# Softmax attention and soft experts on one core: denominators inverted on GpSimd, and one copy moved from ScalarE to VectorE

## The chip, the core and the metric

The kernel runs on one core of a Trainium2 chip. Its time is the device time of one execution in microseconds (us); the time before is the median of three runs. The engines are called as in the profile: PE is TensorE, PEld its weight loads, DVE is VectorE, ACT is ScalarE, POOL is GpSimd, SP is SyncE. Each engine works through its own queue in order and waits at semaphores for the others.

## What is computed

The reference is attention with an extra one in the denominator, followed by a soft mixture of experts on its output.

```python
scores = scale * np.matmul(q, k.transpose(0, 1, 3, 2))      # 8 x 12 heads, 448 tokens, 64 wide
m = np.max(scores, axis=-1, keepdims=True)
e = np.exp(scores - m)
attn = e / (np.sum(e, axis=-1, keepdims=True) + np.exp(-m) + 1e-09)
x = np.matmul(attn, v)                                      # to 3584 x 768
logits = x @ phi                                            # 32 slots
d = softmax of logits over tokens; slot_input = d.T @ x
slot_out = relu(slot_input @ w1[e]) @ w2[e]                 # 8 experts, 4 slots each
out = (softmax of logits over slots) @ slot_out
```

Only the division by attention's denominator and the maxima m of the last heads are touched by the change.

## The kernel before

**Pairs and groups.** The 96 heads are worked in 48 pairs, n = 0 to 47, six pairs to a batch element. The loop over s from 0 to 47 issues the work of several pairs mixed: scores and exponentials of pair s (`AB`, `Bk`), row maxima of later pairs (`A`, `A1`), the product of the probabilities with v for pairs s and s - 1 (`AV`), the normalization of pair s - 1 (`N1`, `N2a`, `N2b`), the transposes of pair s - 2 (`PX`) and, once in six pairs, the steps of the mixture's softmax (`P`). The order within a step is written out by hand in lists of tokens (L700): in a steady step it is 'AB0', 'AV3', 'AB1', 'AVd', 'AVc', 'N1', 'PO0', 'AB2', 'N2a', 'H', 'N2b', 'PO1', 'W', 'AVa', 'PX', 'AVb', 'PO2', 'PO3', 'G'. Since every engine's queue is in order, that list sets who stands behind whom.

**Row maxima.** PE writes scores into PSUM (L302, L294, L284), and DVE reduces each 128x448 tile to a column (L303, L296, L287). When all pairs of a group (three pairs, fewer at the start) have their columns, PE turns them (`W2`, L310 and L313), ACT copies the turned rows from PSUM to `mT` (`W3`, L319) and makes exp(-m) from the columns into `ec` (L324). The scores of the group's pairs then get their maxima subtracted on PE by a second matmul (L380, L354) which reads `mT`, and ACT takes the exponential from PSUM (L382, L357). There are 17 groups; the last is pairs 45 to 47, and its `W3` is issued in step 44.

**Normalization.** v carries a column of ones, so the product with v also gives the sum of e. `N1` copies the product from PSUM to `ubuf` (ACT, L435; DVE for the last pairs). `N2a` adds 1e-9 and `ec` to the sums: one DVE instruction of 128x7 into `rec` (L447). `N2b` inverts `rec` (DVE, L454) and scales: one product of 128x384 (L457) and two of 64x64 (L468). `on_pool(n)` is true for n under 44, and there the products are POOL's; for the last four pairs they are DVE's (ACT has a part in the very last). Between L447 and L454 the list has 'H', which puts one row maximum (L296) and, in two pairs of three, a copy of turned q and k (L265) on DVE's queue.

**After it.** `PX(n)` transposes the normalized pair on PE (L484), one step after its `N2b`; ACT or DVE copies the result to `xT` (L494, L492, L490), and POOL doubles 64 columns (L495).

**What else is on POOL's queue.** The copies of v into the layout with ones (L397 to L400, each third step), the issues of the loads of q and k (L161) and v (L165, L166), of the experts' weights (L111, L131) and of a copy of weights within DRAM (L137), two or three small steps per batch element of the mixture's softmax (L547, L562, L579), and memsets at the start (L217 to L219).

Of the kernel before, what the change touches and what calls it, by code (L numbers as in the profile page):

```python
# [8 lines left out]
F32 = mybir.dt.float32  # L9
# [3 lines left out]
ALU = mybir.AluOpType  # L13
# [19 lines left out]
def kernel(  # L33
# [10 lines left out]
    nc = tc.nc  # L44
    B, H, S, D = q.shape
# [16 lines left out]
    const = ctx.enter_context(tc.tile_pool(name="const", bufs=1))  # L62
# [7 lines left out]
    identf = const.tile([128, 128], F32, name="identf")  # L70
    ident2 = const.tile([128, 128], BF16, name="ident2")
    ones = const.tile([128, 2], BF16, name="ones")
    blocks = const.tile([128, 4], BF16, name="blocks")
    sel = const.tile([128, NP], BF16, name="sel")
    phi_sb = const.tile([128, KC, NS], BF16, name="phi_sb")
# [67 lines left out]
    with ExitStack() as at:  # L143
# [72 lines left out]
        for t in xb:  # L216
            nc.gpsimd.memset(t[:, 3, :], 0.0)  # L217
        nc.gpsimd.memset(ones, 1.0)
        nc.gpsimd.memset(ones[64:128, 1:2], 0.0)  # L219

        ec, mT, eT, av, us = {}, {}, {}, {}, {}
        qkT = {}
        st = {"e2": 0}
# [46 lines left out]
        groups = [range(0, 1), range(1, 3), range(3, 6), range(6, 9), range(9, 12), range(12, 15), range(15, 18), range(18, 21), range(21, 24), range(24, 27), range(27, 30), range(30, 33), range(33, 36), range(36, 39), range(39, 42), range(42, 45), range(45, 48)]  # L270
# [45 lines left out]

        def W3(g):
            t = psm.tile([128, S], BF16, tag="mT", name="mT")
            nc.scalar.copy(t, st["ps_m"][:, 0:S])  # L319
            mT[g] = t  # L320
            e = psm.tile([128, NP, 4, 2], F32, tag="ec", name="ec", bufs=3)
            w = wm[g % 2][:, 0:512].rearrange("p (i c) -> p i c", i=4)
            for h in range(2):
                nc.scalar.activation(e[:, :, :, 1 - h].rearrange("p l i -> p i l"), w[:, :, 64 * h:64 * h + NP],  # L324
                                     AF.Exp, scale=-scale)
            ec[g] = e
# [99 lines left out]
        on_pool = lambda n: n < NPAIR - 4  # L426
# [23 lines left out]
        def N2b(n):  # L450
            b, pb = divmod(n, PB)
            u, rec = us[n], recs[n]
            eng = nc.gpsimd if on_pool(n) else nc.vector
            nc.vector.reciprocal(rec, rec)  # L454
            x = xb[b % 2]
            c = pb * 128
            eng.tensor_mul(  # L457
                x[:, 0:3, c:c + 128].rearrange("p i (h d) -> p i h d", h=2),
                u[:, 0:6, 0:D].rearrange("p (i h) d -> p i h d", h=2),
                rec[:, 0:6].rearrange("p (i h) -> p i h", h=2).unsqueeze(3).to_broadcast([128, 3, 2, D]))  # L460
            if n == NPAIR - 1:
                for h in range(2):
                    r, d = slice(64 - 64 * h, 128 - 64 * h), slice(c + 64 * h, c + 64 * h + 64)
                    nc.scalar.mul(x[r, 3, d], st["av3"][r, 0:D], rec[r, 6:7])
                return
            for h in range(2):
                r, d = slice(64 - 64 * h, 128 - 64 * h), slice(c + 64 * h, c + 64 * h + 64)
                eng.tensor_mul(x[r, 3, d], u[r, 6, 0:D], rec[r, 6:7].to_broadcast([64, D]))  # L468
# [259 lines left out]
        warm(2, 512, 64)  # L728
        W2(0)
        W3(0)  # L730
        As(1)
        T(2)
# [20 lines left out]
        def do(tok, s):  # L753
# [3 lines left out]
            elif tok == "AV3":  # L757
                for i in range(4):
                    AV(s - 1, i, [3])
            elif nm == "AV":  # L760
                i = "abcd".index(tok[2])
                AV(s - i // 2, i, range(3))
            elif tok == "H":
                Bk(s, 3, 1, turned(s + 6, (12, 12, 4)) if s < NPAIR - 6 else ())
            elif tok == "N1":
                N1(s - 1)
            elif tok == "N2a":
                N2a(s - 1)
            elif tok == "N2b":
                N2b(s - 1)  # L770
            elif tok == "PX":
                PX(s - 2)
            elif tok == "W":
                while wnext[0] < len(groups) and (not runs or runs[0][0] > groups[wnext[0]][-1]):
                    W2(wnext[0])
                    W3(wnext[0])
                    wnext[0] += 1
            elif nm == "PO":
                step(s, int(tok[2]))
            elif tok == "G":  # L780
                while later:
                    later.pop(0)()
            elif tok == "X":
                prep()
            elif tok == "P6":
                PX(n6)

        for s in range(NPAIR):
# [3 lines left out]
            for y in range(2 * (s < 3)):  # L792
# [21 lines left out]
                if y == 0:  # L814
                    if s:
                        for i in (2, 3):
                            AV(s - 1, i, range(3))
                        for i in range(4):
                            AV(s - 1, i, [3])
                        N1(s - 1)  # L820
                else:
                    if early and s:
                        N2a(s - 1)
                    if hs > 1:
                        do("W", s)
                    AV(s, 0, range(3))
                    if s == 2:
                        PX(s - 2)
                    if s:
                        N2b(s - 1)  # L830
                    AV(s, 1, range(3))
                    do("G", s)
# [3 lines left out]
            g = (s + 10) // 3  # L836
# [3 lines left out]
            g = (s + 9) // 3  # L840
# [22 lines left out]
        n = NPAIR - 1  # L863
# [6 lines left out]
        N1(n)  # L870
        N2a(n)
        N2b(n)
        nc.gpsimd.memset(mine, 0.0)
        for g in range(2):
# [181 lines left out]
```

## Time and profile before

| | us |
|---|---|
| runs | 287.29, 288.33, 289.04; median 288.33 |
| profiled execution | 287.19, of which the span of instructions is 285.4 |
| busy in the span | PE 262.8, ACT 243.4, DVE 248.4, POOL 191.1 |
| L303, row maxima on DVE | 254 of 0.612 |
| L382, exponentials on ACT | 272 of 0.608 |
| L454, reciprocals on DVE | 48 of 0.187 |
| L447, denominators on DVE | 47 of 0.173 |
| L457, products on POOL | 44 of 0.824; before them POOL was idle for 27.2 in all |
| L468, products on POOL | 88 of 0.287 |
| L319, copies of maxima on ACT | 17 of 0.558 |

A line of the timeline has the start and the length in us, the engine, the line of the kernel, the operation, the tiles written and read with their shapes, and a count if several were merged; in brackets stands how long the engine was idle before it and who ended that. A line of the windows has, for each engine, the busy time in the stretch and the number of instructions; PEclk is the granted clock of TensorE. An instruction's length is not always what it costs its queue: DVE and ACT start the next instruction up to 0.2 us before the last has ended, so costs to a queue are read from start to start. Most of R is one big SBUF buffer that holds many tiles by turns.

### The profile page before, as it was taken

What the parts mean: (1) busy time and instruction counts of PE and PEld (TensorE: products, weight loads), DVE (VectorE), ACT (ScalarE), POOL (GpSimd) and SP (SyncE); (2) the same over time, 40 slices, a digit from 0 to 9 for tenths busy, and PEclk for the clock granted to TensorE, in tenths of its full rate; (3) what the DMA queues carried; (4) which work ended last, traced back from release to release, by engine and by line L of the source; (5) the groups of instructions that cost most, each with busy time, mean ns of one, the idle gap of its engine ahead of it and who ended that gap; (6) DMA issues with size and microseconds to landing.
All of it is one profiled execution on the core that took longest, in us unless ns stands there. A gap on an engine that the chain in (4) does not pass through costs nothing.

```text
span 285.4 us, 11963 instructions
## 1 busy us (share of the span) xinstructions
PE 262.8 (92%) x4967; PEld 151.4 (53%) x4967; DVE 248.4 (87%) x587; ACT 243.4 (85%) x556; POOL 191.1 (67%) x387
## 2 busy tenths in 40 slices
PE   8998999999999999999999999999899999995800
PEld 3455565656565656555665656556555466542100
DVE  6999999999999999999999999999899687438900
ACT  3688999999999999999999999999899996456800
POOL 8868697979688989878888888897757743000000
PEclk9999999999999999999999999999999999998555
DMA  7999999999999999999999999999947999939994
GB/s 135 166 184 157 203 206 205 200 208 181 184 195 209 176 190 201 207 198 172 133 205 162 194 204 209 177 201 203 179 61 110 148 164 233 364 142 364 422 434 199
DMA packets 50214, 57.67 MB, mean 202 GB/s; under 512 B 2928, under 2 KB 42608, under 8 KB 49776
## 3 DMA queue, kind: packets, MB, share of 16 engines
q0 software_dynamic: 45280, 42.29, 95.0%
q1 hardware_dynamic: 4880, 14.62, 13.2%
q8 instruction: 39, 0.64, 0.8%
q14 instruction: 15, 0.12, 0.1%
HBM read 88.18 MB, written 14.16 MB: 359 GB/s over the span
## 4 chain that ended last, share of the span: by engine, by line
PE 60%; DVE 22%; POOL 6%; issue 3%; ACT 3%; DVEq 0%; POOLq 0%
DVE R L303 13%; PE ps_av L422 10%; PE ps_a L302 9%; PE ps_b L377 6%; PE ps_b L380 6%; PE ps_t L237 3%; PE ps_av L414 3%; PE ps_x L484 3%; DVE R L296 2%; PE ps_b L348 2%; PE ps_warm L179 2%; PE ps_o L943 2%; PE ps_so L915 2%; PE ps_l L515 2%; PE ps_h L900 2%
## 5 line engine op out<-in xcount | busy, mean ns | idle before, releaser
L303 DVE TENSOR_REDUCE R<-ps_a 128x1 bf16<-128x448 f32 x254 | 139.9, 612 | 1.7 <-PE ps_a L302 1.1
L382 ACT ACTIVATE R<-ps_b 128x448 bf16<-128x448 f32 x272 | 135.0, 608 | 2.6 <-PE ps_b L380 2.0
L302 PE MATMUL ps_a<-R 64*128 64x448 bf16 x254 | 89.9, 354 | 0.1
L377 PE MATMUL ps_b<-R 64*128 64x448 bf16 x272 | 70.6, 354 | 0.0
L380 PE MATMUL ps_b<-mT,sel 64*128 64x448 bf16 x272 | 68.5, 349 | 0.2 <-ACT mT L319 0.2
L422 PE MATMUL ps_av<-R 128*128 128x65 bf16 (+1 forms) x1248 | 64.7, 196 | 0.6 <-issue 0.4
L422 PEld LDWEIGHTS <-R 128*128 128x128 bf16 (+1 forms) x1248 | 46.7, 101 | 24.1 <-issue 21.9
L457 POOL TENSOR_TENSOR R<-ubuf,rec 128x384 bf16<-128x384 f32 x44 | 36.2, 824 | 27.2 <-DVE rec L454 12.6
L357 ACT ACTIVATE R<-ps_b 128x448 bf16<-128x448 f32 x64 | 37.5, 603 | 2.7 <-PE ps_b L354 2.5
L237 PE MATMUL ps_t<-ident,R 64*64 64x64 bf16 x1344 | 31.1, 195 | 0.3 <-DVE R L287 0.2
L380 PEld LDWEIGHTS <-sel 64*128 64x128 bf16 x272 | 23.9, 94 | 11.2 <-issue 1.6
L468 POOL TENSOR_TENSOR R<-ubuf,rec 64x64 bf16<-64x64 f32 x88 | 25.3, 287 | 6.8
L296 DVE TENSOR_REDUCE R<-ps_a 128x1 bf16<-128x448 f32 x48 | 29.5, 614 | 0.0
L237 PEld LDWEIGHTS <-R 64*64 64x64 bf16 x1344 | 26.3, 110 | 3.4 <-issue 1.6
L302 PEld LDWEIGHTS <-R 64*128 64x128 bf16 x254 | 23.7, 93 | 7.2
L435 ACT COPY ubuf<-ps_av 128x455 f32<-128x455 f32 x44 | 26.6, 604 | 0.0
L494 ACT CAST R<-ps_x 128x448 bf16<-128x448 f32 x41 | 25.0, 611 | 0.0
L348 PE MATMUL ps_b<-R 64*64 64x448 bf16 (+1 forms) x112 | 21.6, 369 | 0.6 <-DVE R L287 0.6
L354 PE MATMUL ps_b<-mT,sel 64*64 64x448 bf16 (+1 forms) x112 | 20.5, 350 | 1.3 <-issue 1.0
L287 DVE TENSOR_REDUCE R<-ps_a 128x1 bf16<-128x448 f32 x34 | 18.7, 614 | 0.7 <-PE ps_a L284 0.6
L951 DVE TENSOR_SCALAR W<-ps_o,ubuf 128x768 f32<-128x768 f32 (+2 forms) x21 | 14.8, 746 | 4.5 <-PE ps_o L943 2.1
L484 PE MATMUL ps_x<-ident,R 128*128 128x128 bf16 x192 | 17.8, 213 | 0.1
(163 smaller groups left out, 470.8 us busy)
## 6 DMA issues: line engine op xcount, KB each, us to landing
W<-in_moe_w_dram POOLq DMA_DIRECT2D x22, 768.0 KB, 10.2
R<-in_v_dram POOLq DMA_DIRECT2D x32, 192.0 KB, 5.6
out_dram<-W SPq DMA_DIRECT2D x2, 2688.0 KB, 10.9
R<-in_q_dram POOLq DMA_DIRECT2D x14, 336.0 KB, 8.9
R<-in_k_dram POOLq DMA_DIRECT2D x14, 336.0 KB, 9.9
wd<-in_moe_w_dram POOLq DMA_DIRECT2D x8, 384.0 KB, 9.9
R<-wd SPq DMA_DIRECT2D x8, 384.0 KB, 7.2
out_dram<-W SPq DMA_DIRECT2D x6, 384.0 KB, 2.9
```

The lines of the kernel that those rows point to most:

```text
L237: nc.tensor.transpose(ps[r, a, c:c + 64], nat["qk"[a], n // NP][f, n % NP, tok * D:(tok + 1) * D], ident[f, f])
L296: nc.vector.reduce_max(top(n, i), ps[:, 0:S], axis=AX.X)
L302: nc.tensor.matmul(ps[:, 0:S], t[r, 0, i * 128:(i + 1) * 128], t[r, 1, :], start=True, stop=True)
L303: nc.vector.reduce_max(top(n, i, hl), ps[:, 0:S], axis=AX.X)
L348: nc.tensor.matmul(outs[hl], t[rs[hl], 1, cols], t[rs[hl], 0, :], start=True, stop=False)
L357: nc.scalar.activation(e, p[:, 0:S], AF.Exp, scale=scale)
L377: nc.tensor.matmul(ps[hl][:, 0:S], t[rs[hl], 1, cols], t[rs[hl], 0, :], start=True, stop=False)
L380: nc.tensor.matmul(ps[hl][:, 0:S], sel[rs[hl], pl:pl + 1].to_broadcast([64, 128]), mT[mg(n)][rs[hl], :], start=False, stop=True)
L382: nc.scalar.activation(e[:, hl, :], ps[hl][:, 0:S], AF.Exp, scale=scale)
L422: nc.tensor.matmul(o, eT[n, i, hl][:, qc], vh[:, h, :], start=(i == 0 and (u == 0 and hl == 0 or u == 3 and n == NPAIR - 1)), stop=(i == 3 ...
L435: (nc.scalar.copy if n1_act(n) else nc.vector.tensor_copy)(u, src)
L457: eng.tensor_mul(x[:, 0:3, c:c + 128].rearrange("p i (h d) -> p i h d", h=2), u[:, 0:6, 0:D].rearrange("p (i h) d -> p i h d", h=2), rec[: ...
```

## The change

The reciprocal of the first 44 pairs goes from DVE to POOL, where it is written as a power: `rec` to the minus one, with the exponents in a tile `minus` of 128x7, set once at the start. It is issued where L454 stood, just ahead of POOL's products. The last four pairs keep DVE's reciprocal. And for the last of the 17 groups the copy of the turned maxima from PSUM is DVE's instead of ACT's.

```diff
+    minus = const.tile([128, 7], F32, name="minus")
...
         nc.gpsimd.memset(ones, 1.0)
+        nc.gpsimd.memset(minus, -1.0)
...
         def W3(g):
             t = psm.tile([128, S], BF16, tag="mT", name="mT")
-            nc.scalar.copy(t, st["ps_m"][:, 0:S])
+            (nc.vector.tensor_copy if g == len(groups) - 1 else nc.scalar.copy)(t, st["ps_m"][:, 0:S])
...
             eng = nc.gpsimd if on_pool(n) else nc.vector
-            nc.vector.reciprocal(rec, rec)
+            if on_pool(n):
+                nc.gpsimd.tensor_tensor(rec, rec, minus, op=ALU.pow)
+            else:
+                nc.vector.reciprocal(rec, rec)
```

## The prediction

> **What bounds the kernel now.** I read the page first, for the totals and for the chain of work that ended last.
>
> ```profile
> PE 262.8 (92%) x4967; PEld 151.4 (53%) x4967; DVE 248.4 (87%) x587; ACT 243.4 (85%) x556; POOL 191.1 (67%) x387
> ...
> PE 60%; DVE 22%; POOL 6%; issue 3%; ACT 3%; DVEq 0%; POOLq 0%
> ```
>
> Three engines are nearly full, and the chain changes between PE and DVE. POOL looks free at 67%, but the chain has 6% on it. So I read the windows next, in one stretch of the attention loop:
>
> ```profile
> core 0: us, PE busy (x) PEld busy (x) DVE busy (x) ACT busy (x) POOL busy (x), PEclk, DMA share, GB/s
> ...
> 121.00:147.00 26.00, 26.00 (x546) 15.65 (x543) 25.52 (x62) 25.78 (x62) 21.25 (x44) 1.00 1.13 174
> ```
>
> Here DVE, ACT and PE leave less than 0.5 us of 26 idle (POOL's 21.25 counts its DMA issues). The loop takes about 4.6 us a pair (from the first L457 at 26.4 to the 44th at 224.8: 198.4 us for 43 pairs), so POOL is free for 4.75 / 5.7 = 0.8 us a pair. Then the timeline of POOL and DVE in one cycle of three pairs, because V's copies and the loads come in cycles of three:
>
> ```profile
> 138.41 0.81 POOL L457 TENSOR_TENSOR R<-ubuf,rec 128x384 bf16<-128x384 f32 x1
> ...
> 140.08 0.80 POOL L111 DMA_DIRECT2D W<-in_moe_w_dram  x1
> 141.59 0.82 POOL L457 TENSOR_TENSOR R<-ubuf,rec 128x384 bf16<-128x384 f32 x1 [0.71 <-ACT ec L324]
> ...
> 145.21 0.54 POOL L562 TENSOR_TENSOR z<-lb,lb 128x160 f32<-128x160 f32 x1
> 146.56 0.83 POOL L457 TENSOR_TENSOR R<-ubuf,rec 128x384 bf16<-128x384 f32 x1 [0.82 <-DVE rec L454]
> ```
>
> ```profile
> 140.12 0.15 DVE L447 SCALAR_TENSOR_TENSOR rec<-ubuf,ec 128x7 f32<-128x7 f32 x1
> 140.19 0.61 DVE L296 TENSOR_REDUCE R<-ps_a 128x1 bf16<-128x448 f32 x1
> 140.72 0.61 DVE L265 COPY R<-ps_t 128x896 bf16<-128x896 bf16 x1
> 141.25 0.18 DVE L454 RECIPROCAL rec<-rec 128x7 f32<-128x7 f32 x1
> 141.36 0.23 DVE L532 TENSOR_REDUCE cm<-lb 128x4 f32<-128x128 f32 x1
> ```
>
> See two things. The reciprocal stands 0.5 to 1.1 us behind the denominator's sum (L447), since a row maximum and, in two pairs of three, a copy are queued between them; it is the reciprocal, not ACT's `ec` of the label, that ended the wait at 141.59 (it ended at 141.43). And the first product of the cycle did not wait at all: POOL came to it 1.3 us late (the reciprocal ended at 137.05), behind V's copies and three DMA issues. Who waits for POOL is in the timeline of the next cycle:
>
> ```profile
> 153.78 0.82 POOL L457 TENSOR_TENSOR R<-ubuf,rec 128x384 bf16<-128x384 f32 x1
> 154.67 0.64 POOL L468 TENSOR_TENSOR R<-ubuf,rec 64x64 bf16<-64x64 f32 x2
> 155.37 0.10 PEld L484 LDWEIGHTS <-R 128*128 128x128 bf16 x1 [0.23 <-POOL R L468]
> ```
>
> PE's fourth transpose of that pair stood until POOL had finished. In the other late pairs the same transposes start 0.5 to 2.1 us after POOL's last product, mostly about 1 us.
>
> **Part one, what DVE loses.** 44 of the 48 reciprocals go (n from 0 to 43; the last four stay on DVE). Each is 0.18 us long, but DVE starts its next instruction 0.11 us after it (141.25 to 141.36). 44 x 0.107 = 4.7 us of DVE's queue. Were DVE the path throughout, all of it would come; were ACT or PE, nothing: 0 to 4.7. In the loop's stretch from 43 to 199 us the chain lies on DVE for about 30% (L303 24.1%, L296 3.8%, L265 and small ones the rest). I take 30% of 4.7 = 1.4 us.
>
> **Part one, what POOL gains.** 44 powers of 128x7, in front of each product. The trace has none. Call P the time that one adds to POOL's queue. From below: POOL's products take 0.287 us at 64 columns and 0.824 at 384, so 1.68 ns a column over 0.18 us; at 7 columns 0.19. The product reads what the power wrote; a copy over a fresh memset (L852, L855) starts 0.07 us after its end. P is at least 0.26. By ratio: POOL against DVE on the same products is 0.287 / 0.220 = 1.30 and 0.824 / 0.558 = 1.48; times the reciprocal's 0.187 that is 0.24 to 0.28, with the gap 0.31 to 0.35. The arithmetic of a power beyond that is not in any row; the longest computation on POOL, 0.92 us, is the upper end that I keep. I take 0.35, nearest to the ratio.
>
> What hides it: the power waits for L447 rather than for L454, so POOL starts earlier wherever it waited. In the cycle shown, L447 had ended (140.27) before POOL came free (140.88), so all of the 0.71 but the usual 0.07 is recovered; at 146.56 the sum ended at 145.78 and POOL was free at 145.75, so 0.82 less 0.15 of signalling. Together 1.3 us in three pairs, 0.43 to 0.45 a pair. While 3P is under that, lateness does not pile up. At 0.35 it does not; only the pair at 153.78, which has no cover, pays about 0.3 us. Above 0.45 each pair adds P - 0.45 to POOL's lateness until the transposes wait each cycle: about 44 x (P - 0.45), less the 1 us of slack that is used up once.
>
> Behind the waiting power on POOL's queue stand the product, L495, the copies of V and the issues of q, k, v and the weights. They stood behind the waiting product already. V's copies are used two pairs later and the loads later still; that is their cover, and without it they would join the same lateness. The memset of `minus` (0.1 us, by L218 and L219) falls into POOL's 0.43 us wait at 11.44: nothing.
>
> **Part two, the last copy of maxima.** From the timeline:
>
> ```profile
> 224.47 0.24 PE L313 MATMUL ps_m<-ident,R 128*128 128x64 bf16 x2
> 224.82 0.55 ACT L357 ACTIVATE R<-ps_b 128x448 bf16<-128x448 f32 x1
> 225.25 0.55 ACT L319 CAST mT<-ps_m 128x448 bf16<-128x448 f32 x1
> 225.39 0.29 DVE L556 TENSOR_REDUCE lb<-ps_bc 128x32 f32<-128x128 f32 x1 [0.76 <-PE ps_bc L555]
> 225.85 0.36 PE L380 MATMUL ps_b<-mT,sel 64*128 64x448 bf16 x2 [0.20 <-ACT mT L319]
> ```
>
> The transposed maxima are in PSUM at 224.71. On ACT the copy stands behind an exponential and ends at 225.80, and PE waits 0.20 for it. DVE is idle from 224.63 to 225.39; its copy of 128x455 took 0.63, so it ends near 225.40, just when L556 could start. That gives PE the 0.20 and ACT 0.41 (the step from L319 to L324) in a stretch where ACT has no idle time: 0.2 to 0.4. I take 0.2.
>
> **Sum.** -1.4 - 0.2 + 0.3 = -1.3 us. The profiled execution took 287.19 us (span 285.4 and 1.8 around it), so 285.9. The median of the runs is 288.33, 1.1 above; with the same step, 287.0.
>
> **The rivals.** (a) *POOL becomes the bound* because a power costs more than 0.45 us. For it: a power is no single product, and POOL is already late once in each cycle. Against it: both ratios. At P = 0.6 the loss is 44 x 0.15 - 1 = 5.6, and what DVE gave is worth nothing: 294 on the median's scale. At 0.9 it is 18.8: 307. If the power is worked through at many times a product's cost, say 2 us, it is 67: 355. This one is slower, with its turn at P = 0.45. Chance 0.40, of which 0.17 beyond 0.9 and 0.04 too small to tell.
>
> (b) *DVE was the bound nearly everywhere*: PE's pieces in the chain are waits for PSUM that DVE frees. For it: reductions follow each other without a gap. Against it: ACT is as full. All 4.7 and 0.4 come: 283.2. Chance 0.08.
>
> (c) *The first power costs extra once*, its code being brought in. The 2.4 us between the first pair's last product and its transposes (28.00 to 30.42) hide as much; beyond that each us adds one. The nearest row is ACT's table load, 1.28 us, which would be hidden, and the first L457 (0.82) was no longer than the rest. For it to matter it must take twice the cover, 4.8 us: then 289.4. Chance 0.05. The Trainium skill's GPSIMD Engine Reference, section 2.1, says that the first call to a freshly loaded kernel pays some 6 us that the profile does not show as an instruction. By that the sum, as an estimate, would be 3.5 us higher, near 290.5. No run here shows it.
>
> **Chances.** The forecast, P from 0.26 to 0.45 with DVE's part between little and most, has 0.47. A difference of 0.5%, about 1.4 us, is what a measurement of this kernel can tell. The forecast lies close to that bound, so I split it: 0.28 faster, 0.19 within. With the rivals: faster 0.28 + 0.08 = 0.36; within 0.19 + 0.04 + 0.05 = 0.28; slower 0.36. The range goes from (b), 283.2, to P = 0.9, 307; the forecast's own range is 284.5 to 288.3.
>
> **What would show it.** In the profile after, the power's row on POOL gives P less its gap; L457 should still show waits before it, now ended by L447; DVE should have 44 instructions fewer and about 4.7 us less work; L484 should wait for L468 no more than once or twice; L380's wait for `mT` near 225 should be gone. I am wrong on the sign if the power takes over 0.4 us, if POOL stands near 100% in the windows, or if PE's weight loads wait for L468 in each cycle.

## The result, and the profile after

The changed kernel takes 334.56 us (median of 4, 332.56 to 335.27) against 288.15 for the kernel before: a ratio of 1.160, 95% interval 1.154 to 1.165, or 46 us slower. The range on record ended at 307. In the changed kernel the line numbers are 1 to 5 higher: the power is L457, the products are L462 and L473, the transposes of `PX` L489, POOL's doubling of 64 columns L500, the mixture's logits L520.

From the page of the changed kernel: the totals, the chain, and the row of the power.

```profile
PE 277.7 (83%) x4966; PEld 157.2 (47%) x4967; DVE 253.6 (76%) x544; ACT 249.2 (75%) x555; POOL 259.4 (78%) x432
...
POOL 40%; PE 32%; DVE 9%; ACT 7%; issue 7%; POOLq 0%; DVEq 0%; ACTq 0%
...
L457 POOL TENSOR_TENSOR rec<-rec,minus 128x7 f32<-128x7 f32 x44 | 66.4, 1509 | 2.9 <-DVE rec L449 0.8
```

POOL's share of the chain went from 6% to 40%. One power of seven columns takes 1.51 us; the reciprocal on DVE took 0.187. Of the 27.2 us that POOL waited ahead of its products, 2.9 are left ahead of the powers and 3.5 ahead of the products. The window of the same stretch as before:

```profile
121.00:147.00 26.00, 21.39 (x402) 12.78 (x396) 18.79 (x41) 19.43 (x46) 24.72 (x41) 0.87 1.09 167
```

DVE, ACT and PE, which had been full, now each idle for 4.6 to 7.2 us of 26, and POOL is the full one. Who waits for it, from POOL's timeline and PE's row at 133 us:

```profile
128.90 0.79 POOL L138 DMA_DIRECT2D wd<-in_moe_w_dram  x1
129.76 1.51 POOL L457 TENSOR_TENSOR rec<-rec,minus 128x7 f32<-128x7 f32 x1
131.35 0.82 POOL L462 TENSOR_TENSOR R<-ubuf,rec 128x384 bf16<-128x384 f32 x1
132.25 0.65 POOL L473 TENSOR_TENSOR R<-ubuf,rec 64x64 bf16<-64x64 f32 x2
132.86 0.23 POOL L500 COPY R<-R 128x64 bf16<-128x64 bf16 x1
133.14 0.21 PE L520 MATMUL ps_l<-phi_sb,R 128*128 128x32 bf16 x1 [3.89 <-POOL R L500]
```

From the power's start to the product's it is 1.59 us: that is what one power adds to POOL's queue. The queue runs without a gap here, and at the end of six of the eight batch elements PE stands until POOL's last doubling: 18.0 us in six waits at L520 (before, at L515, a single weight load waited for POOL, for 0.2 us), beside 12.6 at the transposes L489. From POOL's first 128x384 product to its 44th it is 246.8 us instead of 198.4: the loss lies in the loop.

### The profile page after: what moved, and what is told of

It is laid out like the page before. It is cut to its first block, busy times and chain, and to the rows that moved or that the text cites. A ratio compares the mean times of both kernels' runs of the same rounds, so it can differ in the third digit from the quotient of the medians.

```text
span 332.8 us, 12012 instructions
## 1 busy us (share of the span) xinstructions
PE 277.7 (83%) x4966; PEld 157.2 (47%) x4967; DVE 253.6 (76%) x544; ACT 249.2 (75%) x555; POOL 259.4 (78%) x432
## 4 chain that ended last, share of the span: by engine, by line
POOL 40%; PE 32%; DVE 9%; ACT 7%; issue 7%; POOLq 0%; DVEq 0%; ACTq 0%
POOL rec L457 11%; POOL R L462 6%; POOL R L473 6%; PE ps_av L424 5%; PE ps_a L304 4%; PE ps_b L379 3%; DVE R L289 3%; POOL W L112 3%; PE ps_b L382 3%; POOL R L162 3%; ACT R L384 2%; DVE R L305 2%; POOL R L166 2%; PE ps_so L920 2%; PE ps_h L905 2%
## 5 line engine op out<-in xcount | busy, mean ns | idle before, releaser
L305 DVE TENSOR_REDUCE R<-ps_a 128x1 bf16<-128x448 f32 x254 | 142.1, 619 | 18.9 <-PE ps_a L304 9.9
L384 ACT ACTIVATE R<-ps_b 128x448 bf16<-128x448 f32 x272 | 133.4, 578 | 15.2 <-PE ps_b L382 13.7
L304 PE MATMUL ps_a<-R 64*128 64x448 bf16 x254 | 94.2, 371 | 0.2 <-DVE R L298 0.2
L379 PE MATMUL ps_b<-R 64*128 64x448 bf16 x272 | 75.6, 370 | 1.0 <-DVE R L298 1.0
L382 PE MATMUL ps_b<-mT,sel 64*128 64x448 bf16 x272 | 73.5, 366 | 0.0
L457 POOL TENSOR_TENSOR rec<-rec,minus 128x7 f32<-128x7 f32 x44 | 66.4, 1509 | 2.9 <-DVE rec L449 0.8
L424 PEld LDWEIGHTS <-R 128*128 128x128 bf16 (+1 forms) x1248 | 49.4, 105 | 25.1 <-issue 22.6
L462 POOL TENSOR_TENSOR R<-ubuf,rec 128x384 bf16<-128x384 f32 x44 | 36.4, 827 | 3.5
L359 ACT ACTIVATE R<-ps_b 128x448 bf16<-128x448 f32 x64 | 36.2, 583 | 1.9 <-PE ps_b L356 1.6
L489 PE MATMUL ps_x<-ident,R 128*128 128x128 bf16 x192 | 22.1, 225 | 13.7 <-POOL R L462 6.6
L473 POOL TENSOR_TENSOR R<-ubuf,rec 64x64 bf16<-64x64 f32 x88 | 25.5, 290 | 6.7
L298 DVE TENSOR_REDUCE R<-ps_a 128x1 bf16<-128x448 f32 x48 | 29.6, 617 | 0.0
L520 PE MATMUL ps_l<-phi_sb,R 128*128 128x32 bf16 x192 | 7.5, 177 | 18.0 <-POOL R L500 18.0
L489 PEld LDWEIGHTS <-R 128*128 128x128 bf16 x192 | 13.2, 102 | 18.7 <-POOL R L473 9.1
```

Of the source, the lines that this page charges most:

```text
L304: nc.tensor.matmul(ps[:, 0:S], t[r, 0, i * 128:(i + 1) * 128], t[r, 1, :], start=True, stop=True)
L305: nc.vector.reduce_max(top(n, i, hl), ps[:, 0:S], axis=AX.X)
L359: nc.scalar.activation(e, p[:, 0:S], AF.Exp, scale=scale)
L379: nc.tensor.matmul(ps[hl][:, 0:S], t[rs[hl], 1, cols], t[rs[hl], 0, :], start=True, stop=False)
L382: nc.tensor.matmul(ps[hl][:, 0:S], sel[rs[hl], pl:pl + 1].to_broadcast([64, 128]), mT[mg(n)][rs[hl], :], start=False, stop=True)
L384: nc.scalar.activation(e[:, hl, :], ps[hl][:, 0:S], AF.Exp, scale=scale)
```

## The experiments

Each row of times is a ratio to the kernel before in the same sitting, with its 95% interval; us are the ratio times that sitting's median of before (287.4 to 288.0).

**Parts alone.** Each keeps one of the two edits of the change.

> The powers on GpSimd, the last copy on ScalarE as before. Theory A: 334.8, the whole of the loss, within 0.5 us of the changed kernel. Rival B (part of the loss lies in the moved copy): over 1 us faster than the changed kernel's 334.56.

> Only the last group's copy of maxima is VectorE's; all reciprocals stay on VectorE. Theory A (the power's time on GpSimd's queue is the whole loss): this part is worth 0.2 to 0.4 us, so 287.7 to 288.0 against 288.15, too little for this measurement; in the trace the matmul L380 near 225 no longer waits for mT. Rival B (the moved copy delays VectorE's s_max chain near 225): 0.3 us or more slower, with L556 starting after 225.6.

The power alone: 1.169 (1.165 to 1.174), 48.7 us. It loses as much as the two edits together, so the moved copy has no visible share in the loss. Its median, 335.57, lies 1.0 us above the changed kernel's 334.56, where at most 0.5 was expected; the two were not timed together. The moved copy alone: 1.004 (1.000 to 1.008), so it cannot be told from nothing, and a gain of more than 0.1 us is outside the interval. Yet in its trace the wait that it was to take away is gone:

```profile
225.34 0.24 PE L313 MATMUL ps_m<-ident,R 128*128 128x64 bf16 x2
225.62 0.62 DVE L319 CAST mT<-ps_m 128x448 bf16<-128x448 f32 x1
226.26 0.29 DVE L556 TENSOR_REDUCE lb<-ps_bc 128x32 f32<-128x128 f32 x1
226.35 0.35 PE L380 MATMUL ps_b<-mT,sel 64*128 64x448 bf16 x2
```

From the start of the last L313 to L380 it is 1.01 us instead of 1.38, and L556 starts 0.92 after L313 as before. Rival B, a delayed L556, is not there. The 0.37 us are real at that place; in the whole time no gain shows.

**Is it the power, or the time it takes in the queue?** Three kernels put other work where the power stood.

```diff
# product_7: the same tiles and shape, a plain product
-            nc.vector.reciprocal(rec, rec)
+            if on_pool(n):
+                nc.gpsimd.tensor_tensor(rec, rec, minus, op=ALU.mult)
+            else:
+                nc.vector.reciprocal(rec, rec)
# small_twice: no inversion for n < 44, the two 64x64 products issued twice
-            nc.vector.reciprocal(rec, rec)
+            if not on_pool(n):
+                nc.vector.reciprocal(rec, rec)
...
-                eng.tensor_mul(x[r, 3, d], u[r, 6, 0:D], rec[r, 6:7].to_broadcast([64, D]))
+                for _ in range(1 + on_pool(n)):
+                    eng.tensor_mul(x[r, 3, d], u[r, 6, 0:D], rec[r, 6:7].to_broadcast([64, D]))
# all_twice: as small_twice, and the 128x384 product twice as well
```

> The power replaced by a plain product of the same tiles and shape (128x7) at the same place on GpSimd; the inversion is left out. Queue time per pair by the rows of before: 0.26 us. Theory A: no lateness piles up, so within 1 us of the kernel without any reciprocal, and faster than before. Rival C (a dependent instruction in front of the scaling costs a signalling of 0.5 us or more on GpSimd, whatever it computes): slower than before by over 2 us.

> No inversion for the first 44 pairs, and GpSimd issues its two 64x64 products twice: 0.65 to 0.73 us more queue time a pair, none of it a power. Theory A, with the loss 44 x (P - 0.45) - 1: 7.8 to 11.3 us slower than before, 296 to 299.5. Rival D (the loss comes from the power itself, by a clash with VectorE or by slowing the clock, not from queue time): no more than 2 us slower than before.

> No inversion for the first 44 pairs, and GpSimd issues all three products twice: 0.90 + 0.70 = 1.6 us more queue time a pair, the same as a power takes (1.51 and a gap of 0.08). Theory A: the same time as the changed kernel, 333 to 337. Rival D (the power harms beyond its queue time): clearly below, under 325.

I measured the queue time in each trace as the median, over the 44 pairs, from the start of the first of a pair's instructions to the end of its last product: 1.55 us before. The rest is what was added; it stands for P in the third column.

| kernel | added per pair, us | by 44 x (P - 0.45) - 1 | measured, us (interval) |
|---|---|---|---|
| product_7 | 0.29 | no lateness | -1.0 (-2.0 to -0.1) |
| small_twice | 0.72 | 10.9 | 8.1 (6.7 to 9.5) |
| all_twice | 1.63 | 50.9 | 48.5 (46.7 to 50.3) |
| power_alone | 1.60 | 49.6 | 48.7 (47.5 to 50.0) |

Plain products that fill POOL's queue for as long as a power cost as much as the power. So rival D, harm beyond the queue time, falls, and so does rival C, a dear signalling on POOL. Between the second row and the third, 0.91 us of queue cost 40.4 us: 44 per us, one for each pair. The chain of small_twice, then that of all_twice, show POOL taking over:

```profile
POOL 39%; PE 29%; DVE 15%; issue 5%; DMA 4%; ACT 2%; DVEq 0%; POOLq 0%; SPq 0%
```

```profile
POOL 49%; PE 21%; DVE 14%; issue 5%; DMA 5%; ACT 1%; DVEq 0%; POOLq 0%
```

**The budget.** The power for some pairs only, the reciprocal for the rest (`if on_pool(n) and n % 3 == 1:`, or `n % 6 == 1`).

> The power on GpSimd only for pairs with n % 3 = 1 (15 of the first 44), the pair whose product waited 0.7 us for the reciprocal; the other reciprocals stay on VectorE. Theory A, by budget: GpSimd can take up to 1.35 us in a cycle of three pairs, and one power is 1.6; the excess of 0.25 to 0.3 a cycle piles up to about 4 us in 14 cycles, less 1 us of slack: 290 to 292. Rival E (each power costs its 1.6 us less 0.45 where it stands, with no help from the pairs beside it): 15 x 1.15 - 1 = 16, 304. Rival F (lateness within a cycle is hidden as long as the transposes' own 1 us of slack holds): no difference.

> The power only for pairs with n % 6 = 1 (8 of the first 44). Theory A, by budget: 1.6 us in six pairs against 2.7 that GpSimd can take; the lateness is made up before the next one: within 0.7 us of before. Rival E: 8 x 1.15 - 1 = 8, 296.

One in three: 1.013 (1.007 to 1.018), 3.6 us, where the budget said 2 to 4, rival E 16 and rival F nothing. One in six: 1.004 (1.001 to 1.007), 1.0 us, a little over the 0.7 expected but far from E's 8. The lateness of one power is made up by the waits of the pairs beside it as long as there are enough of them.

**What a power costs.** On a scratch tile, behind POOL's last instruction of the kernel before. (The power with plus one was not in the kernel that ran.)

> The kernel before, with powers and products on a scratch tile on GpSimd, put behind its last instructions, four of each shape: powers of 128 partitions by 1, 2, 4, 7, 14 columns, of 16, 4 and 1 partitions by 7, a product of 128x7, and a power with plus one as the exponent. Theory A1 (a routine that works on all partitions together, some 0.19 us a column over a start of 0.16): 0.36, 0.55, 0.93, 1.51, 2.86 us, and 1.51 for 16, 4 and 1 partitions too; product 0.19; the exponent changes nothing. Rival A2 (a large fixed price, some 1.2 us, whatever the width): 1.2 to 1.5 at all widths up to 7. Rival A3 (the partitions of a share are worked through one by one): 1 and 4 partitions take far less than 16.

The sources' rows give the shortest, the median and the longest in ns:

```profile
L888 POOL TENSOR_TENSOR pr<-pr,pe x4: 548/556/577, 239.9 to 241.8; 128x1 f32<-128x1 f32 x4
L890 POOL TENSOR_TENSOR pr<-pr,pe x4: 691/694/722, 242.4 to 244.8; 128x2 f32<-128x2 f32 x4
L894 POOL TENSOR_TENSOR pr<-pr,pe x4: 1477/1478/1478, 249.9 to 254.6; 128x7 f32<-128x7 f32 x4
L896 POOL TENSOR_TENSOR pr<-pr,pe x4: 2584/2586/2586, 256.1 to 264.1; 128x14 f32<-128x14 f32 x4
L902 POOL TENSOR_TENSOR pr<-pr,pe x4: 1468/1468/1468, 279.2 to 283.8; 1x7 f32<-1x7 f32 x4
L904 POOL TENSOR_TENSOR pr<-pr,pe x4: 198/204/207, 285.4 to 286.2; 128x7 f32<-128x7 f32 x4
```

The first five are powers, the last is a product. From 1 to 14 columns a power grows by (2.586 - 0.556) / 13 = 0.156 us a column over a start of 0.40. A1 had the column dearer and the start cheaper; A2's fixed price is out, and so is A3's share by share: one partition takes as long as 128 (4 and 16 took 1.468 as well). The product of the same 128x7 takes 0.204, as the line through the products of before gave (0.19). Even one column of power, 0.56 us, is over the 0.45 that POOL had to spare.

**Why DVE's relief brought nothing.** The prediction had 1.4 us for it.

```diff
# no_reciprocal: the inversion is left out for n < 44
-            nc.vector.reciprocal(rec, rec)
+            if not on_pool(n):
+                nc.vector.reciprocal(rec, rec)
# reciprocal_twice
+            if on_pool(n):
+                nc.vector.reciprocal(twice, rec)
             nc.vector.reciprocal(rec, rec)
# fewer_exps; both_less has this and the edit of no_reciprocal
+            if g:
+                ec[g] = ec[0]
+                return
```

> The inversion of the first 44 pairs is left out altogether (GpSimd multiplies by the denominators). It prices what VectorE's 44 reciprocals cost on the path, and GpSimd's earlier start, with nothing added to GpSimd. The prediction's term says 1.4 us (286.7); if VectorE bounds the loop nearly everywhere, 4.7 us (283.4); if ScalarE and TensorE hold it, under 0.5 us.

> VectorE makes each of the first 44 reciprocals twice, the extra one into a tile that nobody reads: 44 x 0.107 = 4.7 us more on VectorE's queue, the same amount that the change takes away, and GpSimd's start 0.1 us later. If VectorE is a bound in some 30% of the loop, as the prediction had it: 1.4 us slower. If it is bound by ScalarE and TensorE alone, as the run without reciprocals says: within 0.6 us of before. If VectorE binds throughout: 4.7 us.

> ScalarE makes the exponentials exp(-m) for the denominators only for the first group and all later groups use those (this leaves out 32 of 34; the denominators are then not the reference's): 32 x 0.11 = 3.6 us less on ScalarE's queue; VectorE keeps its reciprocals. If ScalarE alone holds the loop: 2 to 3.6 us faster (284.4 to 286). If VectorE or TensorE holds it as well: within 0.7 us of before.

> As the run before, and the first 44 inversions left out too: 4.7 us less on VectorE and 3.6 us less on ScalarE. If VectorE and ScalarE bound the loop together, each of them just behind the other, the two reliefs bring what neither brings alone: 2 to 3.6 us faster (284.4 to 286). If TensorE's own queue is the bound that is left: within 0.7 us of before, as each alone.

Without the reciprocals: 1.000 (0.998 to 1.002), -0.1 us; 4.7 us of DVE's queue and an earlier start on POOL, for nothing. With each made twice: 1.017 (1.014 to 1.020), 4.9 us. That looks like the whole of 4.7, but the expectation had mispriced it: in the trace the second of the two starts 0.227 us after the first, and DVE's queue grew by 0.227 + 0.118 - 0.107 = 0.24 a pair, 10.5 us, of which about half came out. POOL's products also start that much later, and the run does not tell the two apart. With ScalarE relieved alone: 1.001 (0.998 to 1.005). With both relieved: 0.996 (0.993 to 1.000), 1.1 us out of 4.7 and 3.6. That is short of the 2 to 3.6 that a joint bound of the two would have given, and its interval, 0.1 to 2.1 us, takes in the 0.7 of the other case. The chain of no_reciprocal, then of reciprocal_twice:

```profile
PE 67%; DVE 16%; POOL 3%; ACT 3%; DMA 3%; issue 2%; DVEq 0%; POOLq 0%
```

```profile
DVE 59%; PE 24%; POOL 7%; issue 2%; ACT 2%; DVEq 0%; POOLq 0%
```

With less on DVE, the chain goes over to PE; with more, DVE takes it. That fits three engines of nearly equal load, of which PE would be the floor. This is argued from the chains: no run relieved PE, and what in PE's order would hold it (its own work, or the waits before its weight loads that the profile gives to "issue") was not tried.

**A candidate for a faster kernel.** The reciprocal moved right behind the sum, and the last copy on DVE.

```diff
# in N2a, behind L447; L454 is taken out
+            nc.vector.reciprocal(recs[n], recs[n])
```

> A candidate for a faster version: the reciprocal stays on VectorE but stands right behind the sum L447, ahead of the row maximum and the copy; and the last copy is VectorE's. GpSimd may start each product 0.5 to 1.1 us earlier. VectorE pays some 0.12 us a pair because the reciprocal then reads what the instruction just before it wrote (0.19 from L447 to L454 in the last pairs, 0.07 to L296 in the others). If GpSimd's lateness counts in the kernel before (the wait at 155.37), up to 0.5 us faster; if VectorE's queue bounds, 44 x 0.12 x 0.3 = 1.5 us slower.

1.006 (1.002 to 1.009), 1.6 us slower. This kernel has the moved copy too, which alone measured 1.004 (1.000 to 1.008) beside the same runs of before, so the part of the moved reciprocal cannot be told from nothing. No gain from POOL's earlier start shows; DVE pays for it with 0.191 us from L447 to the reciprocal that reads its result, where L296 started after 0.073 before. No version measured here that computes the reference's result beats the kernel before.

## Why the prediction was wrong

**The step that failed** is the price of the power: "I take 0.35, nearest to the ratio". It measured 1.59. The ratios of POOL to DVE were those of products, and held for products (0.204 for 128x7). A power is another computation, with 0.156 us a column where a product of the kernel before has 0.0017. The upper end failed too: "the longest computation on POOL, 0.92 us, is the upper end that I keep". A row of one operation bounds nothing about another; with no row of a power, no upper end could be had from the trace, and the range should have gone as far as rival (a)'s 2 us.

**The consequence of P was right.** The bound of 0.43 to 0.45 us a pair, read from one cycle of three pairs, and the slope of 44 us per us put all kernels with more work on POOL within about 3 us. With 1.59 in place of 0.35 the working gives 49 us; 46 and 49 were measured. All losses lie below what it gives; as an estimate, a bound of 0.47 to 0.51 would have met them, so one cycle was a fair sample and not an exact one. Rival (a) is what happened, with a chance of 0.40. Its three signs all came: the power takes 1.51 us, POOL is busy for 24.72 of 26 us, and PE's weight loads of L489 waited for POOL 26 times.

**That POOL would start earlier was right.** In the page of before, POOL's waits ahead of the pair's first instruction are ended most by the reciprocal; in product_7 by L449, the sum (us and times):

```profile
L457 POOL TENSOR_TENSOR R<-ubuf,rec 128x384 bf16<-128x384 f32 x44 | 36.2, 824 | 27.2 <-DVE rec L454 12.6
```

```profile
  DVE rec L449: 8.5, 12
```

**DVE's 1.4 us was wrong**: -0.1 (-0.7 to 0.5). I had taken DVE's share of the chain, 30%, for its share of what a relief brings. A chain tells who is last now, not by how much; by the chain of no_reciprocal, PE stood right behind.

**The moved copy** gave its 0.2 to 0.4 at the place named, without delay to L556. On the whole time it did not show.

**The first power** (rival c) cost nothing extra: 1.52 us at 25.89, as the rest. Some 6 us that the Trainium skill's GPSIMD Engine Reference (section 2.1) gives for the first call to a freshly loaded kernel are not seen here: POOL waited 0.22 us ahead of the power, for the sum, and the product starts 1.60 us after the power, as in later pairs.

**One thing was not foreseen**: the transposes were named as the place of the wait, and most of PE's time for POOL was lost at L520, where the logits read what POOL doubled last. By the working it changes no number, since POOL's queue sets both.

## What to carry to other kernels

Before work goes to an engine that looks free, read how much time it has between the points where others wait for it (here 0.45 to 0.5 us a pair, though it was idle for a third of the span), and price the new operation by a run of that operation: an operation without a row in the trace has no upper bound. The share of an engine in the chain is no measure of what its relief brings when two others are as full. Plain work of the same length in the same place tells at once whether an operation harms by its time alone.

## What was not expected of the hardware

Where POOL's lateness left PE idle, the granted clock of PE fell to half, for 3.4 or 6.8 us. Three stretches of the changed kernel, ahead of, at and behind the wait at L520:

```profile
128.00:132.00 4.00, 1.25 (x57) 0.99 (x49) 1.91 (x5) 1.34 (x4) 3.85 (x5) 0.93 1.10 119
132.00:135.00 3.00, 1.86 (x23) 1.67 (x23) 0.28 (x1) 1.42 (x5) 2.82 (x6) 0.50 0.90 146
135.00:139.00 4.00, 4.00 (x37) 1.68 (x36) 3.11 (x7) 2.38 (x6) 3.77 (x8) 0.59 1.24 204
```

PEclk, third from the end, is 0.93, 0.50, 0.59: PE got half its clock just when it had work again. There were seven such drops ahead of 250 us in the changed kernel, six in all_twice, and none in small_twice. In the trace of the changed kernel PE had been busy for 9 to 55% of the 3.41 us ahead of each drop; stretches of 57% and more had none (in power_alone one of 50% had none either). The Trainium skill's page "TensorE: Matmul & The Clock Gate" (Part 1) has the half clock after an idle window of about 3.4 us; here half a window was enough, and a single gap of 1.7 us (61.62 to 63.33). all_twice has the drops too, so they come of the idle PE and not of the power. What they cost was not measured, but it is a small part of the 46 us: POOL's queue sets the loop's time, and of POOL's waits over 0.2 us in the loop only two stand in or just behind a drop, that from 237.25 to 244.07:

```profile
244.64 0.52 POOL L567 TENSOR_TENSOR z<-lb,lb 128x160 f32<-128x160 f32 x1 [1.99 <-DVE lb L563]
245.76 1.50 POOL L457 TENSOR_TENSOR rec<-rec,minus 128x7 f32<-128x7 f32 x1 [0.61 <-DVE rec L449]
```
